# Two splits of the next token group one slot earlier, and four more units in the other product order, in a fused attention + two-MLP kernel

## The chip, the core and the metric

The kernel runs on one core of a Trainium2 chip. TensorE (PE) does the matrix products, ScalarE (ACT), VectorE (DVE) and GpSimd (POOL) do the work between them, SyncE (SP) issues the DMAs. The metric is the device time of one execution in microseconds; less is better.

## The reference, cut to what matters

```python
def _attn_ref(q, k, v):                       # 4 batches, 8 heads, 576 tokens, head size 64
    ...                                       # attention inside chunks of 64 tokens
    attn = np.exp(scores)
    attn = attn / (np.sum(attn, axis=-1, keepdims=True) + 1e-09)
    out = np.matmul(attn, v_c)
...
def _moe_ref(x, w_in, w_out):                 # x: 2304 x 512; w_in: 512 x 2048
    h = np.maximum(x @ w_in, 0.0)
    return (h * h @ w_out).astype(np.float32)
...
def _moe2_ref(x, domain_probs, w1, w2):       # 4 experts, w1[e]: 512 x 1024, w2[e]: 1024 x 512
    ...
    for e in range(E):
        h = np.maximum(x @ w1[e], 0.0)
        out += p[:, e:e + 1] * (h @ w2[e])
```

The attention output is the first MLP's input, and that MLP's output is the input of the four experts.

## The kernel before, in words

Attention and the first MLP fill roughly the first 485 us. The change lies in the last part, the experts.

**Split numbers.** A float32 operand is kept as a high part (a cast to fp32r, on ACT) and a low part (operand minus high part, on POOL or DVE), and a product is three matmuls: high by high, high by low, low by high.

**Units and slots.** The tokens are three groups of 768, each the left and right half of a 2x2 block matrix. A unit is 256 hidden columns of one expert for one group: 16 units a group, n = 0 to 47. From unit 7 on each layer uses Strassen's scheme (in Winograd's form), with seven products in place of eight. A unit has seven slots, u = 0 to 6, written here as (n, u). In slot (n, u) PE first runs one first-layer product of unit n (`c_unit`, line 609: 6 matmuls of 384 columns) and then three second-layer products (`d_unit`, line 710: 9 matmuls of 256 columns), of unit n-1 where u is 1 to 6 and the last three of unit n-2 where u is 0. So a slot is 15 matmuls.

**First layer.** The seven token operands (Y11, Y21, Y22, T1 to T4) stand split in seven places of one buffer. `UNITS` fixes their use: slot 0 takes Y11, then Y21, T2, T1, T3, Y22, T4. For a new group each place must be rewritten after the last unit of the old group (n = 15, 31) read it and before the first unit of the new one does. `SPLITS` says after which slot that is done: a key below 7 is a slot of the group's last unit, a key from 7 on is slot key-7 of the unit after. The rewrite (`y_split`) is an ACT cast at line 425 and a subtraction at line 427, on DVE for Y11, Y21, Y22 and on POOL for T1 to T4.

**Second layer.** The hidden block is turned into A11, A12, A22 and sums S1 to S4. The splits of the sums are an ACT cast (line 634) and a POOL subtraction (line 635); S2 itself is made by POOL (line 666). `PRODUCTS` lists the seven products; (t, k) in `SLOTS` is product k for token tile t of 3. Products 1, 2, 3, 5 of a tile go to one PSUM bank, 4, 6, 7 to another. DVE or ACT empty those banks in the middle of the accumulation: "B" (lines 763, 765) reads the bank of 6 and 7 before product 4 is added to it, "A" (line 767) reads the bank of 1 and 5 before products 2 and 3 are added to it. `AFTER` and `AFTER_ONCE` say after which slot each is recorded.

**The other product order.** A unit whose number is in `ONCE` takes `SLOTS_ONCE` and `AFTER_ONCE`: tile 0 and tile 1 begin with product 1 in place of product 7, so that the low part of S3 and S2 is asked for one product (3 matmuls) later; and of tile 2, products 6 and 1 come one slot later, with B and A of tile 2 both recorded after slot 6 in place of slots 5 and 6.

**Order.** The instruction streams of all engines are written out by hand in the loop at lines 1009 to 1081 (`manual_schedule`); each engine runs its own stream in order, and semaphores hold an instruction until what it reads is there and what it overwrites has been read. In a slot the order of recording is: `c_unit`, the unit's `c_finish`, `d_unit`, the moves, and last the splits.

Of the kernel before, what the change touches and what calls it, by code (L numbers as in the profile page):

```python
# [48 lines left out]
def tile_kernel(ctx, tc, q, k, v, moe_w_in, moe_w_out, moe2_p, moe2_w1, moe2_w2, out):  # L49
# [328 lines left out]
    Y11, Y21, Y22, T1, T2, T3, T4 = range(7)  # L378
# [43 lines left out]
    def y_split(sp, i):  # L422
        h, l = y_slot(i)
        a = comb[sp][i]
        nc.scalar.copy(h, a)
        eng = nc.vector if sp == 0 or i in (Y11, Y21, Y22) else nc.gpsimd
        eng.tensor_tensor(out=l, in0=a, in1=h.bitcast(F32), op=ALU.subtract)  # L427
        yield
# [267 lines left out]
        ((0, 5), (1, 5), (0, 4)), ((1, 4), (0, 2), (0, 3)), ((1, 2), (1, 3), (2, 7)),  # L696
        ((2, 1), (2, 6), (2, 5)),
    )
    ONCE = (9, 10, 13)
    pb = {}  # L700

    def d_unit(n, t, k):
        si, wi, x, c = PRODUCTS[k]
        if k in (1, 7):
            pb[n, t, x] = bank("a")
        p = pb[n, t, x][:, c * 2 * P:(c + 1) * 2 * P]
        hi, lo = (y[:, t * P:(t + 1) * P] for y in g[n][si])
        bh, bl = (y[:, wi] for y in w2c[n])
        for z, (w, y) in enumerate(((hi, bh), (hi, bl), (lo, bh))):
            nc.tensor.matmul(  # L710
                p, lhsT=w, rhs=y, start=(k in (1, 7) and z == 0), stop=(k in (3, 4) and z == 2),
                skip_group_check=True,
            )
# [107 lines left out]
    }  # L821
    AFTER_ONCE = {**AFTER, 5: ((1, "O"),), 6: ((2, "B"), (2, "A"))}
    ENDS = (3, 4, 0, 1, 5, 2)
    SPLITS = {1: Y11, 3: T2, 4: T1, 5: Y21, 8: T3, 9: Y22, 10: T4}

# [37 lines left out]
    with tc.manual_schedule():  # L865
# [44 lines left out]
        def run(chunks, n=None):  # L910
            while n is None or n > 0:
                try:
                    next(chunks)
                except StopIteration:
                    return
                n = None if n is None else n - 1
# [92 lines left out]
        for n in range(NQ + 2):  # L1009
# [5 lines left out]
            for u in range(7):  # L1015
# [54 lines left out]
                for d, at_ in ds:  # L1070
                    if 0 < at_ < 8:
                        for t, k in (SLOTS_ONCE if d in ONCE else SLOTS)[u]:
                            d_unit(d, t, k)
                    for t, what in (AFTER_ONCE if d in ONCE else AFTER if d < NQ - 2 else FLUSH).get(at_, ()):
                        d_move(d, t, what)
                if n < NQ and u == 4:
                    low(n, A22, st[n, "c"][:, :HALF])
                for back in (0, 1):
                    s1, m1 = divmod(n - back, NU)
                    if n >= back and m1 == NU - 1 and s1 + 1 < NSUP and u + 7 * back in SPLITS:  # L1080
                        run(y_split(s1 + 1, SPLITS[u + 7 * back]))

# [24 lines left out]
```

## Time and profile before

| what | value |
|---|---|
| median of 3 runs | 1200.18 us (1200.11 to 1201.43) |
| the profiled execution: time | 1208.68 us |
| the profiled execution: span of its instructions | 1206.9 us |
| mean granted TensorE clock | 0.994 |
| PE busy | 1185.9 us, 98% of the span |
| DVE, POOL, ACT busy | 841.1, 730.0, 610.4 us |

The span is from the first to the last instruction. A busy PE means that a matmul is in flight; how far apart matmuls start is seen in counts for a stretch and in the start times of a timeline.

### The profile page before, as it was taken

The numbers are of one execution on the slowest core, as the hardware profiler recorded it, in microseconds if no ns is written. First come the engines' busy times: TensorE is split into PE (matmuls) and PEld (weight loads), VectorE is DVE, ScalarE is ACT, GpSimd is POOL, SyncE is SP. The second block draws the span as 40 slices with busy tenths as digits, with TensorE's granted clock in tenths as the row PEclk, the third lists the DMA queues.
The fourth block names the chain that finished last, engine by engine and source line by source line (L and its number), as shares of the span: only waits on it lengthen the run. The fifth ranks groups of instructions, "written<-read, shape, count | busy, mean of one in ns | idle before, by whom it ended". The sixth has DMA issues, their size and how long they took to land.

```text
span 1206.9 us, 21703 instructions
## 1 busy us (share of the span) xinstructions
PE 1185.9 (98%) x8128; PEld 1110.9 (92%) x8128; DVE 841.1 (70%) x1400; ACT 610.4 (51%) x1250; POOL 730.0 (60%) x715
## 2 busy tenths in 40 slices
PE   6799999999999999999999999999999999999998
PEld 5788889888988988988899999999999999999997
DVE  6975665667667676456576778676767786767686
ACT  5655555454455444644354556454545554545543
POOL 3410047676675868777266678666766775656665
PEclk8999999999999999999999999999999999999999
DMA  9955132872964686566766667666666677666661
GB/s 208 198 116 128 44 99 79 278 252 81 327 213 149 217 272 226 201 224 239 291 258 245 247 253 289 257 250 254 249 254 250 252 281 276 262 266 251 246 262 53
DMA packets 142249, 265.43 MB, mean 220 GB/s; under 512 B 65344, under 2 KB 116544, under 8 KB 136000
## 3 DMA queue, kind: packets, MB, share of 16 engines
q1 hardware_dynamic: 139520, 263.39, 62.4%
q8 instruction: 64, 1.05, 0.3%
q10 hardware_dynamic: 2624, 0.66, 0.3%
q14 instruction: 41, 0.34, 0.1%
HBM read 200.58 MB, written 63.44 MB: 219 GB/s over the span
## 4 chain that ended last, share of the span: by engine, by line
PE 93%; DVE 2%; POOL 2%; DMA 1%; issue 1%; ACT 1%; SPq 0%; ACTq 0%; DVEq 0%; POOLq 0%
PE pst L609 23%; PE psa L710 22%; PE psa L336 17%; PE pst L303 10%; PE psh L303 7%; PE psa L727 6%; PE psh L609 4%; PE pst L279 1%; PE pst L238 1%; PE pst L223 1%; DMA v<-in_v 1%; POOL ar L427 1%; PE pst L265 1%; DMA q<-in_q 0%; POOL o L779 0%
## 5 line engine op out<-in xcount | busy, mean ns | idle before, releaser
L609 PE MATMUL pst<-ar 128*128 128x384 f32 x1728 | 347.5, 337 | 0.0
L609 PEld LDWEIGHTS pst<-ar 128*128 128x128 f32 x1728 | 292.1, 188 | 3.6
L336 PE MATMUL psa<-ar 128*128 128x512 f32 (+1 forms) x960 | 218.0, 371 | 0.0
L635 POOL TENSOR_TENSOR ar<-s,ar 128x384 fp32r<-128x384 f32 x160 | 163.3, 1033 | 68.3 <-ACT ar L634 65.2
L336 PEld LDWEIGHTS psa<-ar 128*128 128x128 f32 x960 | 173.8, 188 | 23.1 <-DVE acc L353 0.2
L710 PE MATMUL psa<-w2x,ar 128*128 128x256 f32 x1260 | 169.4, 279 | 0.3 <-POOL ar L635 0.3
L710 PE MATMUL psa<-ar 128*128 128x256 f32 x1260 | 169.0, 279 | 0.6 <-ACT uw L763 0.6
L710 PEld LDWEIGHTS psa<-ar 128*128 128x128 f32 x1260 | 164.7, 188 | 0.9 <-ACT uw L763 0.8
L710 PEld LDWEIGHTS psa<-w2x,ar 128*128 128x128 f32 x1260 | 164.8, 188 | 0.7 <-POOL ar L635 0.6
L779 POOL TENSOR_TENSOR o<-o,x 128x256 f32<-128x256 f32 x114 | 89.4, 784 | 88.5 <-ACT x L775 88.5
L148 POOL TENSOR_TENSOR raw<-raw 128x512 f32<-128x512 f32 x32 | 34.9, 1089 | 171.6 <-DVE raw L147 73.3
L303 PE MATMUL pst<-ar 128*128 128x512 f32 (+1 forms) x576 | 127.2, 369 | 0.0
L634 ACT CAST ar<-s 128x384 fp32r<-128x384 f32 x160 | 82.1, 513 | 81.8 <-DVE s L630 75.1
L642 ACT COPY u<-pst 128x384 f32<-128x384 f32 x144 | 69.5, 483 | 97.8 <-PE pst L609 96.0
L303 PEld LDWEIGHTS pst<-ar 128*128 128x128 f32 x576 | 105.4, 188 | 14.3
L767 DVE TENSOR_TENSOR uw<-psa,uw 128x512 f32<-128x512 f32 x120 | 79.2, 687 | 50.4 <-PE psa L710 29.9
L653 ACT ACTIVATE ar<-psh 128x384 fp32r<-128x384 f32 x96 | 47.3, 492 | 121.8 <-DVE psh L649 67.8
L303 PE MATMUL psh<-ar 128*128 128x512 f32 (+1 forms) x384 | 89.7, 376 | 2.1 <-DVE ar L287 2.1
L303 PEld LDWEIGHTS psh<-ar 128*128 128x128 f32 x384 | 69.1, 190 | 10.7 <-DVE ar L287 2.3
L765 DVE TENSOR_TENSOR uw<-psa,uw 128x512 f32<-128x512 f32 x87 | 59.9, 688 | 23.4 <-PE psa L710 22.1
L485 POOL TENSOR_TENSOR jsplit<-jraw,jsplit 128x448 fp32r<-128x448 f32 x44 | 54.7, 1249 | 35.3 <-ACT jsplit L483 31.0
L476 POOL TENSOR_TENSOR jraw<-jraw 128x256 f32<-128x256 f32 x88 | 70.1, 817 | 1.8
(139 smaller groups left out, 1943.9 us busy)
## 6 DMA issues: line engine op xcount, KB each, us to landing
ar<-w1d SPq DMA_DIRECT2D x41, 1792.0 KB, 7.3
w2x<-w2d SPq DMA_DIRECT2D x40, 896.0 KB, 8.0
ar<-w2d SPq DMA_DIRECT2D x40, 896.0 KB, 8.3
w2d<-jsplit SPq DMA_DIRECT2D x64, 448.0 KB, 4.2
w1d<-ar SPq DMA_DIRECT2D x7, 1792.0 KB, 8.7
w1d<-jsplit SPq DMA_DIRECT2D x24, 448.0 KB, 3.9
raw<-in_moe_w_in SPq DMA_DIRECT2D x16, 512.0 KB, 5.6
raw<-in_moe_w_out SPq DMA_DIRECT2D x16, 512.0 KB, 5.3
```

The source lines that it names most:

```text
L303: nc.tensor.matmul(ph[:, :T], lhsT=w[:, kk, :], rhs=x[tb][:, kk, :], start=(kk == 0 and n == 0), stop=(kk == KD - 1 and n == 2),)
L336: nc.tensor.matmul(o, lhsT=w, rhs=y, start=(f == 0 and n == 0), stop=(f == G - 1 and n == 2))
L476: nc.gpsimd.tensor_tensor(out=r[:, o], in0=r[:, a], in1=r[:, b], op=op)
L609: nc.tensor.matmul(p, lhsT=w[:, kk, :], rhs=y[:, kk, :], start=(kk == 0 and z == 0 and u in (0, 1, 3)), stop=(kk == 1 and z == 2 and u in ...
L634: nc.scalar.copy(h, st[n, nm])
L635: nc.gpsimd.tensor_tensor(out=l, in0=st[n, nm], in1=h.bitcast(F32), op=ALU.subtract)
L642: nc.scalar.copy(s, d if at == 3 else b)
L710: nc.tensor.matmul(p, lhsT=w, rhs=y, start=(k in (1, 7) and z == 0), stop=(k in (3, 4) and z == 2), skip_group_check=True,)
L727: nc.tensor.matmul(p, lhsT=w[:, ts], rhs=y[:, i, :], start=(i == 0 and z == 0), stop=(i == 1 and z == 2))
L765: nc.vector.tensor_tensor(out=uw, in0=b, in1=uw, op=ALU.add)
L767: nc.vector.tensor_tensor(out=uw, in0=pb[n, t, 0], in1=uw, op=ALU.add)
L779: nc.gpsimd.tensor_tensor(out=o1[:, :2 * P], in0=o1[:, :2 * P], in1=x, op=ALU.add)
```

## The change: what it does

```diff
-    ONCE = (9, 10, 13)
+    ONCE = (9, 10, 13, 17, 18, 33, 34)
...
-    SPLITS = {1: Y11, 3: T2, 4: T1, 5: Y21, 8: T3, 9: Y22, 10: T4}
+    SPLITS = {1: Y11, 2: T2, 3: T1, 5: Y21, 8: T3, 9: Y22, 10: T4}
```

No instruction is added or removed on any engine. Four things move, each at both group boundaries (units 15 and 31): the splits of T2 and T1, and the second-layer products and moves of units 17, 18 (and 33, 34).

POOL's stream in unit 15 (acc_1090 holds T1 and T2; x is a scaled output piece that line 779 adds to the output tile; lines 666 and 635 begin the S2 and S3 of unit 15):

```order
 L635 TENSOR_TENSOR ar<-s_7371,ar 128x384
 L787 TENSOR_TENSOR o<-o,x_7385 128x512
-L427 TENSOR_TENSOR ar<-acc_1090,ar 128x768
-L779 TENSOR_TENSOR o<-o,x_7459 128x256
-L427 TENSOR_TENSOR ar<-acc_1090,ar 128x768
-L779 TENSOR_TENSOR o<-o,x_7485 128x256
+L427 TENSOR_TENSOR ar<-acc_1090,ar 128x768 x2
+L779 TENSOR_TENSOR o<-o,x_7461 128x256
+L779 TENSOR_TENSOR o<-o,x_7487 128x256
 L666 TENSOR_TENSOR s_7502<-s_7498,a_7399 128x384
 L635 TENSOR_TENSOR ar<-s_7500,ar 128x384
```

The second subtraction passes the first addition; both splits stand ahead of both additions.

ACT's stream in the same unit (acc_1963 holds Y11; line 642 copies a first-layer bank, 653 and 657 make A22):

```order
 L425 CAST ar<-acc_1963 128x768
 L642 COPY u_7424<-pst 128x384
-L642 COPY u_7446<-pst 128x384
-L775 ACTIVATE x_7459<-psa,prob 128x256
 L425 CAST ar<-acc_1090 128x768
-L653 ACTIVATE ar<-psh 128x384
-L657 ACTIVATE a_7473<-psh 128x384
-L775 ACTIVATE x_7485<-psa,prob 128x256
+L642 COPY u_7448<-pst 128x384
+L775 ACTIVATE x_7461<-psa,prob 128x256
 L425 CAST ar<-acc_1090 128x768
```

T2's cast moves ahead of the copy and the scaled move of slot 3; T1's moves ahead of the two activations and the scaled move of slot 4.

PE's stream in slots 1 to 3 of unit 18, which run the second layer of unit 17 (each psa number is one bank; before, tile 0's bank of products 7 and 6 is psa_7950, after it is psa_7954):

```order
 L609 MATMUL psh_7935<-ar_79 128x384 x6
-L710 MATMUL psa_7950<-w2x_6022,ar_79 128x256 x6
-L710 MATMUL psa_7957<-w2x_6022,ar_79 128x256 x3
-L609 MATMUL pst_7910<-ar_79 128x384 x6
-L710 MATMUL psa_7971<-w2x_6022,ar_79 128x256 x6
-L710 MATMUL psa_7978<-w2x_6022,ar_79 128x256 x3
-L609 MATMUL pst_7983<-ar_79 128x384 x6
-L710 MATMUL psa_7957<-w2x_6022,ar_79 128x256 x3
-L710 MATMUL psa_7978<-w2x_6022,ar_79 128x256 x3
 L710 MATMUL psa_7950<-w2x_6022,ar_79 128x256 x3
+L710 MATMUL psa_7954<-w2x_6022,ar_79 128x256 x6
```

The product that needs no sum (k = 1) now opens the slot, and products 7 and 6 follow it.

## Rows read from the trace of the kernel before

**Rows 1.** Windows: stretch, length; then busy us (matmuls) of PE, PEld, DVE, ACT, POOL.

```profile
740.00:960.00 220.00, 220.00 (x1558) 220.00 (x1557) 159.37 (x268) 112.88 (x254) 146.08 (x147) 1.00 0.67 256
990.00:1190.00 200.00, 200.00 (x1458) 200.00 (x1458) 145.92 (x248) 103.90 (x234) 125.82 (x135) 1.00 0.64 247
```

**Rows 2.** Timeline, PE, 722 to 731: start, length, what; idle time before it.

```profile
721.73 1.19 PE L710 MATMUL psa<-ar 128*128 128x256 f32 x9
722.75 1.20 PE L609 MATMUL pst<-ar 128*128 128x384 f32 x6
...
725.85 0.73 PE L710 MATMUL psa<-w2x,ar 128*128 128x256 f32 x5
726.85 0.74 PE L710 MATMUL psa<-w2x,ar 128*128 128x256 f32 x4 [0.27 <-POOL ar L635]
727.43 1.22 PE L609 MATMUL pst<-ar 128*128 128x384 f32 x6
```

**Rows 3.** Timeline, PE, 960 to 968.

```profile
963.81 1.47 PE L710 MATMUL psa<-w2x,ar 128*128 128x256 f32 x9
965.11 1.20 PE L609 MATMUL pst<-ar 128*128 128x384 f32 x6
```

**Rows 4.** Timeline, PE, 980 to 989.

```profile
982.63 0.85 PE L710 MATMUL psa<-ar 128*128 128x256 f32 x6
984.06 0.62 PE L710 MATMUL psa<-ar 128*128 128x256 f32 x3 [0.58 <-ACT uw L763]
```

**Rows 5.** Timeline, POOL, 700 to 740.

```profile
714.62 2.02 POOL L787 TENSOR_TENSOR o<-o,x 128x512 f32<-128x512 f32 x1
718.10 1.85 POOL L427 TENSOR_TENSOR ar<-acc,ar 128x768 fp32r<-128x768 f32 x1 [1.45 <-ACT ar L425]
...
720.61 1.85 POOL L427 TENSOR_TENSOR ar<-acc,ar 128x768 fp32r<-128x768 f32 x1
...
723.84 1.01 POOL L666 TENSOR_TENSOR s<-s,a 128x384 f32<-128x384 f32 x1
724.81 2.96 POOL L635 TENSOR_TENSOR ar<-s,ar 128x384 fp32r<-128x384 f32 x3
```

**Rows 6.** Timeline, ACT, 705 to 735.

```profile
717.19 0.82 ACT L425 CAST ar<-acc 128x768 fp32r<-128x768 f32 x1
```

**Rows 7.** Timeline, DVE, 714 to 732.

```profile
722.16 1.12 DVE L427 TENSOR_TENSOR ar<-acc,ar 128x768 fp32r<-128x768 f32 x1
723.20 0.68 DVE L767 TENSOR_TENSOR uw<-psa,uw 128x512 f32<-128x512 f32 x1
```

**Rows 8.** Source line 803, DVE: duration ns min/median/max.

```profile
L803 DVE SCALAR_TENSOR_TENSOR o<-uw,prob,o x27: 735/843/3890, 622.0 to 1197.7; 128x512 f32<-128x512 f32 x27
```

**Rows 9.** Timeline, POOL, 950 to 990.

```profile
976.45 1.99 POOL L635 TENSOR_TENSOR ar<-s,ar 128x384 fp32r<-128x384 f32 x2
...
980.07 0.72 POOL L779 TENSOR_TENSOR o<-o,x 128x256 f32<-128x256 f32 x1
```

**Rows 10.** Timeline, DVE, 972 to 986.

```profile
977.46 3.89 DVE L803 SCALAR_TENSOR_TENSOR o<-uw,prob,o 128x512 f32<-128x512 f32 x1
```

**Rows 11.** Timeline, PE, 707 to 713.

```profile
709.23 1.33 PE L710 MATMUL psa<-w2x,ar 128*128 128x256 f32 x9
710.39 1.20 PE L609 MATMUL psh<-ar 128*128 128x384 f32 x6
```

**Rows 12.** Timeline, PE, 662 to 670.

```profile
665.84 1.30 PE L710 MATMUL psa<-ar 128*128 128x256 f32 x9
666.98 1.20 PE L609 MATMUL psh<-ar 128*128 128x384 f32 x6
668.01 1.19 PE L710 MATMUL psa<-w2x,ar 128*128 128x256 f32 x9
```

**Rows 13.** Timeline, PE, 648 to 655.

```profile
650.92 1.30 PE L710 MATMUL psa<-w2x,ar 128*128 128x256 f32 x9
652.06 1.22 PE L609 MATMUL psh<-ar 128*128 128x384 f32 x6
```

## The prediction

> **What bounds the kernel now.** I read the page first: PE is busy for 98% of the span (table above), so an edit pays only where PE waits or where its matmuls start farther apart than they could. In the expert part the waits are few, so I went on to PE's timeline slot by slot and compared start times.
>
> Three waits stand out. In slot (16,1) the second-layer part runs from 725.85 to the next slot's start at 727.43, 1.58 us against the 1.02 of the slot before (721.73 to 722.75); the timeline names POOL's line 635, and by its place (after five of nine matmuls) it is the low part of S2 of unit 15 [rows 2]. In (32,1), one group later, the same part takes 1.30, where 1.06 is usual around it (below) [rows 3]. In (33,3) its first six matmuls take 1.43, some 0.75 too long by six ninths of 1.02, and the wait is for ACT's copy at line 763 [rows 4].
>
> The second thing is larger. Between 740 and 960 PE ran 1558 matmuls in 220 us, between 990 and 1190 it ran 1458 in 200 us, both without a gap, at a granted clock of 1.00 [rows 1]. Per slot of 15 matmuls that is 2.118 against 2.058 us. The instructions have the same shapes. So PE has two paces, 0.060 us a slot apart, and the change from one to the other happens at a short wait: before (16,1) the second-layer part of a slot took 1.02; 0.060 is 0.004 a matmul, so nine take 1.06 at the slow pace, and that stays so for 237.7 us (727.43 to 965.11, 112 slots), until the wait in (32,1), behind which the quick pace is back [rows 2, 3]. Also slow to quick went it in slot (12,0), where 1.14 is followed by a first-layer part of 1.03 [rows 12]. (11,0) lost 0.08 and stayed slow, (15,0) lost 0.14 and stayed quick, (33,3) lost 0.75 and stayed quick [rows 13, 11, 4]. The rows show that a wait can change the pace, not what decides it.
>
> **T2 and T1 one slot sooner.** POOL goes into the boundary late: it ends line 787 at 714.62 + 2.02 = 716.64 and then stands idle 1.45 us until ACT's cast of T2 is there (717.19 + 0.82 = 718.01) [rows 5, 6]. From 718.10 it works through: two subtractions of 1.85, the additions of line 779 (0.72 us undisturbed [rows 9]), S2's making at 723.84, and then three subtractions of 0.99 each from 724.81, of which S2's is the second and ends at 726.79, where PE goes on at 726.85 [rows 2, 5]. After the change T2's cast needs only its own place free, which slot (15,2) has read by 713.5 (it starts five slots of 2.06 before 722.75, and its first-layer part takes 1.04 [rows 2]), and T1's cast takes the place at 717.19 that T2's had. So POOL's first subtraction starts at 716.64, the second at 718.45 (its cast is there at 718.01), two additions end near 721.7, and S2 can be made some two microseconds sooner; DVE's S1, which it needs, is made before DVE turns to the split at 722.16 [rows 7]. S2's low part is 1.3 to 2.2 us sooner, against a lateness of 0.56. Both waits go: 0.56 + 0.24 = **-0.80 us**. ACT's two casts cost nothing: ACT is idle for about half of the span (table).
>
> What is late next? In (16,0), product (2,2) overwrites what the move A (line 767) of tile 2 reads, and A stands behind DVE's split of Y21 (722.16, 1.12 us); it ends at 723.88 [rows 7]. The second-layer part of (16,0) starts one slot before 725.85, at 723.79 [rows 2], and (2,2) is three matmuls in, at 724.13. The cover is 0.25 us, less the release. In the profiled run DVE's subtraction waited for POOL's second one to end (720.61 + 1.85 = 722.46) and ran some 0.82 from there [rows 5, 7]. With POOL ahead, it would find the making of S2 (1.01) under way and start near 722.65, ending 0.19 later: a loss of 0 to 0.2 us a boundary, of which I take 0. DVE can wait longer: line 803, also with two operands in SBUF, took 3.89 us in place of 0.84, from 977.46 to 981.35, while POOL ran one instruction after the other from 976.45 to 980.79 [rows 8 to 10]. I use that for a rival.
>
> The Trainium skill, "SBUF — State Buffer", "Who interferes with whom", says that a VectorE instruction with two SBUF inputs contends with a GpSimd one that reads SBUF, and that the later of the two is blocked until the first is done. It speaks against moving POOL's work under that split. By it the wait is one POOL instruction and the sum is as above; the 3.89 us at line 803 reaches over several, so trace and page differ on how long it can be.
>
> **Four units in the other order.** The order relieves POOL's S3 and S2 by three matmuls (0.34 us). Units 17, 18, 33, 34 show no wait there: slots (18,1), (19,1), (34,1) and (35,1) lie in the two stretches in which PE was busy throughout [rows 1]. So nothing is won. What it costs is seen at the units that have it: B and A of tile 2 now both follow slot 6, and (2,4) and (2,2) wait for them in the next unit's slot 0. Unit 9 lost 0.08 in (11,0), unit 10 0.08 in (12,0), unit 13 0.14 in (15,0) (1.16 against 1.02) [rows 11 to 13]. Four more of them, in (19,0), (20,0), (35,0), (36,0): 0.3 to 0.6, I take **+0.45 us**.
>
> **The pace.** If the wait in (16,1) is gone, what sent PE into the slow pace is gone, and the slots to (32,1) keep the quick one: 112 x 0.060 = **-6.7 us**. The new short waits in (19,0) and (20,0) come in the same place of a slot as those that left a quick pace quick once (15,0) and turned a slow one quick once (12,0), so they favour it. The bounds are 0 (the pace turns slow anyway, or never was) and -6.7.
>
> The wait in (33,3) follows from the 3.89 us above, since the copy it waits for stands behind DVE's late work; POOL's shift moves it out of that coincidence or not. 0 to -0.75, I take 0.
>
> **Sum.** -0.80 + 0.45 - 6.7 = -7.05. The profiled execution took 1208.68 us, so it would be 1201.6. The three runs shown have a median of 1200.18, 8.5 us below the profiled one; taking off the same microseconds gives **1193.1 us**. Its own range is 1192.2 (the (33,3) wait gone too, 0.3 for the orders) to 1194.9 (0.6 for the orders, and quick only from (20,0) on, 26 slots later). I call within 0.2% (2.4 us) no change, about what a measurement of this kernel can tell.
>
> **Rivals.** First, **the pace does not change**: the sum is -0.35, 1199.8 us. For it: the runs shown are 8.5 us shorter than the profiled one. Slow slots there add up to 6.7 us in units 16 to 32, and there are more before (12,0) (650.92 to 665.84 is 14.92 us for seven slots with one loss of 0.08, so 2.12 each [rows 12, 13]); if the runs shown had none of them, there is nothing to win. Against it: the profiled run's early part, loading weights, can as well be what is longer. The Trainium skill, "TensorE: Matmul & The Clock Gate", "Back-to-back issue gap", gives the spacing by the number of columns alone; by that rule there would be no second pace and this would be the result, but [rows 1] show two for the same columns. Chance 0.36.
>
> Second, **slower, the pace turns the other way**: one of the new waits in (35,0) or (36,0) does in the last group what (16,1) did, quick to slow. From (36,0) to the end of unit 46 are 77 slots, +4.6 us; with the third quarter as it was, 1200.18 - 0.35 + 4.6 = 1204.4. It decides as soon as more slots turn slow than quick by 46 (2.4 us plus 0.35). For it: one of three waits met in quick pace did that [rows 2, 4, 11]; against it, the other order's own wait in (15,0) did not. Chance 0.11.
>
> Third, **slower, DVE is starved** at the split of Y21 as at line 803: 3.89 from 722.16 ends at 726.05, A at 726.7, and (2,2) starts 2.6 us late, at two boundaries 5.2; without a gain in pace 1200.18 - 0.35 + 5.2 = 1205.0. It decides once it costs more than 1.4 us a boundary. For it, POOL now runs without a break from 716.64; against it, the split waited for one POOL instruction alone before [rows 5, 7]. Chance 0.08.
>
> **Numbers.** Forecast 0.45, no change of pace 0.36, slower 0.11 + 0.08. Forecast is faster by over 0.2%, the second within, the others slower: 0.45, 0.36, 0.19. Two cases of different sign hold most of the chance, so the range has both, from 1191.0 (1192.2 less the 1.3 us by which the three runs differ, rounded) to 1202.5 (the upper end of no change), and leaves out the slower ones.
>
> **What will show it.** Right: in (16,1) and (32,1) PE's second-layer part takes 1.02 with no wait for line 635; POOL's line 427 starts near 716.6 and 718.4 in place of 718.1 and 720.6 (counted from the same slot); slots of 2.06 from unit 16 to 32; waits of about 0.1 in (19,0), (20,0), (35,0), (36,0). Wrong: slots of 2.12 over that stretch again, or in units 36 to 46; a wait of PE for line 767 or 763 in (16,0) or (32,0); a DVE line 427 of over 2 us in unit 15 or 31; or a trace as forecast and a time that has not moved, which would say that the pace of the profiled execution is not that of the runs.

## The result

In its first timing the changed kernel was slower: a median of 1206.08 us over 11 runs (1203.0 to 1210.7) against 1200.11 for before (1197.22 to 1201.82), ratio 1.0053 with an interval of 1.0043 to 1.0063. A gain of 0.6% was forecast. Yet the profiled execution of the changed kernel (1204.86 us, one of the 11) is shorter than the one the prediction was worked out from (1208.68). That one lies 7 us above every run of before in this timing. Most of what sets either of them apart from later traces of its kernel is PE's pace, as the sum below shows; the sign of the first timing did not come back in the later ones.

The page of the changed kernel, busy time by engine:

```profile
PE 1185.6 (99%) x8128; PEld 1110.8 (92%) x8128; DVE 839.3 (70%) x1400; ACT 610.9 (51%) x1250; POOL 731.2 (61%) x715
```

PE is busy as before, 99% of the span (98% there). Its timeline at the boundary, the changed kernel's answer to [rows 2] (all slots here start 2.9 us earlier than there):

```profile
719.87 1.20 PE L609 MATMUL pst<-ar 128*128 128x384 f32 x6
720.90 1.31 PE L710 MATMUL psa<-ar 128*128 128x256 f32 x9
722.05 1.21 PE L609 MATMUL psh<-ar 128*128 128x384 f32 x6
723.10 1.20 PE L710 MATMUL psa<-w2x,ar 128*128 128x256 f32 x9
724.14 1.20 PE L609 MATMUL pst<-ar 128*128 128x384 f32 x6
...
729.30 1.29 PE L710 MATMUL psa<-w2x,ar 128*128 128x256 f32 x9
730.43 0.85 PE L609 MATMUL pst<-ar 128*128 128x384 f32 x4
```

The second-layer part of (16,1) runs from 723.10 to 724.14, 1.04 us where it was 1.58: the wait for line 635 is gone, as forecast. Two small ones have come. (16,0) takes 1.15 (720.90 to 722.05) and (16,4) 1.13 (729.30 to 730.43), where 1.02 is usual. POOL and DVE show why, in the order POOL, then DVE:

```profile
711.74 2.02 POOL L787 TENSOR_TENSOR o<-o,x 128x512 f32<-128x512 f32 x1
713.71 3.69 POOL L427 TENSOR_TENSOR ar<-acc,ar 128x768 fp32r<-128x768 f32 x2
717.33 1.46 POOL L779 TENSOR_TENSOR o<-o,x 128x256 f32<-128x256 f32 x2
718.71 1.05 POOL L666 TENSOR_TENSOR s<-s,a 128x384 f32<-128x384 f32 x1
...
726.29 1.85 POOL L427 TENSOR_TENSOR ar<-acc,ar 128x768 fp32r<-128x768 f32 x1
```

```profile
719.28 1.31 DVE L427 TENSOR_TENSOR ar<-acc,ar 128x768 fp32r<-128x768 f32 x1
720.51 0.68 DVE L767 TENSOR_TENSOR uw<-psa,uw 128x512 f32<-128x512 f32 x1
...
727.12 1.84 DVE L427 TENSOR_TENSOR ar<-acc,ar 128x768 fp32r<-128x768 f32 x1 [0.37 <-ACT ar L425]
728.88 1.28 DVE L767 TENSOR_TENSOR uw<-psa,uw 128x512 f32<-128x512 f32 x2
```

POOL's two splits run back to back from 713.71, 4.14 us after (15,2) starts at 709.57; in [rows 5] it was 5.65 (718.10 against 712.45), and the forecast was 4.19. (The prediction's 718.45 and 722.65 go by 1.81 us from one start to the next, not by the 1.85 that it prints; the trace has 3.62 for the two splits.) DVE's split of Y21 takes 1.31 in place of 1.12, so A ends at 721.19 and PE's (2,2) waits some 0.1 for it. The split of Y22 that is recorded after (16,2) (727.12, 1.84 us) runs beside POOL's split of T3 (726.29), and the moves A of tiles 0 and 1 behind it are late for (16,4). Each of these DVE splits ends 0.82 to 0.83 us after the POOL instruction that was under way when it began (719.76 to 720.59, 728.14 to 728.96; before, 722.46 to 723.28), which fits a wait for that one instruction and no more; the third rival's 3.89 us did not come. The first of these two waits was in the prediction with 0 to 0.2 us, the second was not in it.

Now the pace. Windows of the changed kernel (the columns of [rows 1], then granted clock, DMA share and GB/s):

```profile
735.00:763.00 28.00, 28.00 (x206) 28.00 (x205) 22.23 (x37) 15.35 (x35) 17.55 (x18) 1.00 0.83 313
780.00:1000.00 220.00, 220.00 (x1558) 220.00 (x1558) 162.05 (x271) 114.91 (x257) 149.98 (x150) 1.00 0.67 257
1030.00:1175.00 145.00, 145.00 (x1057) 145.00 (x1056) 108.72 (x184) 75.13 (x170) 91.51 (x99) 1.00 0.67 258
```

1057 matmuls in 145 us are 2.058 us a slot, 1558 in 220 us are 2.118: the same two paces, to the third digit. The slow stretch has moved. It begins and ends here:

```profile
763.39 1.20 PE L609 MATMUL pst<-ar 128*128 128x384 f32 x6
764.42 1.34 PE L710 MATMUL psa<-w2x,ar 128*128 128x256 f32 x9
765.60 1.22 PE L609 MATMUL psh<-ar 128*128 128x384 f32 x6
766.66 1.22 PE L710 MATMUL psa<-ar 128*128 128x256 f32 x9
767.72 1.22 PE L609 MATMUL pst<-ar 128*128 128x384 f32 x6
```

```profile
1001.00 1.22 PE L609 MATMUL pst<-ar 128*128 128x384 f32 x6
1002.06 1.30 PE L710 MATMUL psa<-w2x,ar 128*128 128x256 f32 x9
1003.20 1.20 PE L609 MATMUL psh<-ar 128*128 128x384 f32 x6
1004.24 1.19 PE L710 MATMUL psa<-ar 128*128 128x256 f32 x9
1005.26 1.02 PE L609 MATMUL pst<-ar 128*128 128x384 f32 x5
```

The first-layer part of (19,0) takes 1.03 (763.39 to 764.42), that of (19,1), behind the wait that unit 17's new order brings (1.18 in place of 1.02), 1.06. The wait of unit 33's order in (35,0) turns it back: 1.06 ahead of it (1001.00 to 1002.06), 1.04 behind. In between lie 112 slots.

### The profile page after: what moved, and what is told of

It is laid out like the page before. It is cut to its first block, busy times and chain, and to the rows that moved or that the text cites. A ratio compares the mean times of both kernels' runs of the same rounds, so it can differ in the third digit from the quotient of the medians.

```text
span 1203.1 us, 21705 instructions
## 1 busy us (share of the span) xinstructions
PE 1185.6 (99%) x8128; PEld 1110.8 (92%) x8128; DVE 839.3 (70%) x1400; ACT 610.9 (51%) x1250; POOL 731.2 (61%) x715
## 3 DMA queue, kind: packets, MB, share of 16 engines
q8 instruction: 64, 1.05, 0.3%
## 4 chain that ended last, share of the span: by engine, by line
PE 96%; DMA 1%; DVE 1%; issue 0%; ACT 0%; ACTq 0%; SPq 0%; DVEq 0%
PE pst L609 25%; PE psa L710 24%; PE psa L336 17%; PE pst L303 10%; PE psh L303 6%; PE psa L727 6%; PE psh L609 4%; DMA k<-in_k 1%; PE pst L279 1%; PE pst L238 1%; PE pst L223 1%; PE pst L265 0%; PE psa L279 0%; PE psa L223 0%; DVE e L245 0%
```

## The experiments

Each timing from the second on ran on a chip of its own, beside runs of before on that chip; on which the first ran is not on record. Medians in us, range in brackets:

| timing | before | kernels |
|---|---|---|
| first | 1200.1 (1197.2 to 1201.8), 11 runs | changed 1206.1 (1203.0 to 1210.7) |
| second | 1199.8 (1197.3 to 1203.2), 29 | splits alone 1199.3 (1197.4 to 1214.3), orders alone 1200.4 (1199.3 to 1202.4), changed without 33, 34: 1201.5 (1198.9 to 1212.4) |
| third | 1199.6 (1197.9 to 1202.3), 18 | changed 1200.3 (one run), tile 2 as usual 1212.2 (1199.5 to 1214.4), changed without 17, 18: 1206.0 (1197.7 to 1215.5), fewer waits 1206.2 (1204.9 to 1212.4) |
| fourth | 1206.2 (1198.0 to 1214.9), 35 | changed 1200.7 (1199.6 to 1203.4), wait put back 1202.3 (1199.3 to 1204.8), tiles 0 and 1 with old splits 1205.4 (1197.4 to 1212.3), moved at 15 only 1201.1 (1199.8 to 1202.4) |
| fifth | 1199.3 (1197.2 to 1208.0), 23 | changed 1198.7 (1197.7 to 1201.7), splits alone 1201.2 (1197.3 to 1206.0) |
| sixth | 1199.8 (1197.3 to 1205.9), 23 | changed 1199.8 (1197.5 to 1202.0), orders alone 1200.6 (1198.1 to 1204.7) |
| seventh | 1199.4 (1198.2 to 1204.4), 23 | changed 1200.3 (1198.4 to 1202.7), tile 2 as usual 1200.6 (1197.5 to 1204.8) |

**The second timing: which part of the change?** The kernel before once more, then each part alone, then the changed kernel without half of its reordered units:

```diff
 splits alone:                 ONCE = (9, 10, 13)
                               SPLITS = {1: Y11, 2: T2, 3: T1, 5: Y21, ...}
 orders alone:                 ONCE = (9, 10, 13, 17, 18, 33, 34)
                               SPLITS = {1: Y11, 3: T2, 4: T1, 5: Y21, ...}
 changed without 33, 34:       ONCE = (9, 10, 13, 17, 18)
                               SPLITS = {1: Y11, 2: T2, 3: T1, 5: Y21, ...}
```

> The kernel before, profiled once more. The page that the prediction rests on took 1208.68 us, above all eleven runs of before (1197.2 to 1201.8). If its slow stretch of 112 slots was that execution's own, this one takes about 1200 us and PE keeps slots of 2.06 us through units 16 to 32 (pace theory: the shown execution was an odd one). If the runs are shorter for another reason (the early part), the slots there are 2.12 us again and the loss lies before 485 us.

It took 1199.64. Its windows, to set against [rows 1]:

```profile
740.00:960.00 220.00, 219.73 (x1599) 219.53 (x1598) 163.23 (x276) 117.57 (x262) 152.01 (x154) 1.00 0.70 265
990.00:1180.00 190.00, 190.00 (x1384) 190.00 (x1384) 139.33 (x237) 97.51 (x220) 119.99 (x129) 1.00 0.63 241
```

1599 matmuls where the first profile of before has 1558, in the same 220 us: no slow slot, though the waits of 0.53 in (16,1) and (32,1) are there. So the execution from which the prediction was made is not what before usually did: no run of the first timing is over 1202, and one of 29 in this timing is over 1203.

> T2 and T1 one slot sooner, the product orders as before. Pace theory (the short waits that the other order brings in (19,0), (20,0), (35,0), (36,0) turn the pace, and that is the 6 us): no such waits here, so the time is that of before or up to 0.8 us less, ratio 0.999 to 1.001, and units 17 to 31 of 14.42 us. Split theory (POOL's work one slot sooner makes DVE's split of Y21 late, and the new wait in (16,0) turns or delays PE): the whole loss, ratio about 1.005. Plain sum of waits: ratio 0.999 to 1.000.

Ratio 1.0003 (0.998 to 1.0026): eleven of the twelve executions lie at 1197.4 to 1200.1, one at 1214.3. Split theory falls; what costs 15 us in that one execution had no trace.

> Units 17, 18, 33, 34 in the other order, the splits as before. Pace theory: the wait in (19,0) or (20,0) turns PE slow until a later wait turns it back ((32,1) or (35,0)), so some 91 to 112 slots of 0.060, ratio 1.004 to 1.006, and units 20 to 31 of 14.84 us in the trace. Split theory: ratio 1.000. Plain sum of waits: four of 0.08 to 0.14 us, ratio 1.0004.

Ratio 1.0006 (0.9995 to 1.0017). Its four new waits are in the trace, some 0.1 each, and none of them turned the pace for longer than a slot. So the waits of the new order need not do what they did in the changed kernel's first trace: pace theory, as stated here, was too simple.

> The changed kernel with 33 and 34 back in the usual order. Pace theory: the wait in (19,0) or (20,0) turns PE slow, and the waits in (35,0) and (36,0) that turned it back in the changed kernel's trace are gone, so it stays slow to unit 46 unless another wait turns it: up to 27 units of 0.42 us, 11 us, ratio up to 1.010, in no case below that of the changed kernel (1.005). Plain sum of waits: half of the changed kernel's four waits, so less than the changed kernel, ratio 1.000 to 1.003.

Ratio 1.0027 (1.0007 to 1.0047), executions from 1198.9 to 1212.4. It is not above the changed kernel's 1.0053, against pace theory as stated. The one with a trace, 1201.62, turned quick in (12,0) and behind that was slow for no more than a slot; what made others take up to 1212.4 is not known.

**The third timing: without the waits.** The order of tile 2 kept, half of the reordered units, and a version with fewer waits:

```diff
 tile 2 as usual:   +SLOTS_EARLY = SLOTS[:1] + SLOTS_ONCE[1:3] + SLOTS[3:]   # for 17, 18, 33, 34
 without 17, 18:     ONCE = (9, 10, 13, 33, 34)
 fewer waits:        ONCE = ()
                     SPLITS = {1: Y11, 2: T2, 3: T1, 4: Y21, 7: Y22, 8: T3, 10: T4}
```

> The changed kernel, profiled once more. Pace theory: its time lies in the range of its eleven runs (1203 to 1211 us) and the excess over 1199 us is in the expert part as slots of 2.12 us between one short wait and another, some 70 to 190 of them; the first of these slots follows a short wait, and its place is not the one of the first trace (units 19 to 35) by necessity. Plain sum of waits: all slots of 2.06 us and the excess in single waits of PE.

Pace theory had it in the range of the first timing and misses: it took 1200.27, below all eleven. Units 17 to 46 ran at 14.42 to 14.57 us, but for unit 32 (14.68) with its two waits. The changed kernel can be as quick as before.

> The changed kernel, but units 17, 18, 33, 34 take the other order for tiles 0 and 1 alone; tile 2 and its moves B and A keep their slots, so PE doesn't wait for A in (19,0), (20,0), (35,0), (36,0). Pace theory: no such waits, no turns of the pace beyond those of the splits alone, ratio 0.998 to 1.001. If the order of the products itself (banks, weights) costs, the ratio is that of the changed kernel, 1.005.

A miss for both theories: median 1212.22, ratio 1.0083 (1.0053 to 1.0113), with none of the four waits. Its timeline in unit 16:

```profile
730.25 1.20 PE L609 MATMUL pst<-ar 128*128 128x384 f32 x6
731.28 1.31 PE L712 MATMUL psa<-w2x,ar 128*128 128x256 f32 x9
732.43 1.22 PE L609 MATMUL pst<-ar 128*128 128x384 f32 x6
733.49 1.22 PE L712 MATMUL psa<-w2x,ar 128*128 128x256 f32 x9
734.55 1.22 PE L609 MATMUL pst<-ar 128*128 128x384 f32 x6
```

The small wait in (16,4) (731.28 to 732.43) turned the pace: first-layer parts of 1.03 ahead, 1.06 behind. From there to unit 46 no slot has a wait, and none is quick.

> The changed kernel with 17 and 18 back in the usual order, so that of the new waits of slot 0 only (35,0) and (36,0) are left, with at most 83 slots behind them. Pace theory: at most 83 x 0.060 = 5 us over before, in some of the executions, ratio 1.000 to 1.004. Plain sum of waits: ratio 0.999 to 1.000.

Ratio 1.0054 (1.0019 to 1.0088): six executions at 1197.7 to 1200.7 and six at 1211.3 to 1215.5, nothing between. Pace theory allowed 5 us and misses. The profiled one, 1212.99, is slow in all 280 slots from unit 8 to the last, so from before the first wait that the change touches; its windows:

```profile
740.00:960.00 220.00, 220.00 (x1560) 220.00 (x1559) 159.44 (x269) 112.56 (x253) 147.84 (x149) 1.00 0.67 255
990.00:1180.00 190.00, 190.00 (x1346) 189.97 (x1346) 134.83 (x229) 95.11 (x215) 114.25 (x123) 1.00 0.66 255
```

> A version that should beat both: T2 and T1 one slot sooner as in the change, DVE's split of Y21 one slot sooner still (so that the move A of tile 2 isn't behind it and (16,0) has no wait), the split of Y22 two slots sooner (so that the moves A after slot 3 aren't behind it and (16,4) has no wait), and no unit in the other order, so no wait in (11,0), (12,0), (15,0) either. Pace theory: hardly a wait is left that can turn the pace, so nearly all executions lie at the quick end, 1196.5 to 1199 us, ratio 0.997 to 0.999, and the spread is smaller than before's. Plain sum of waits: 0.8 + 3 x 0.12 less, ratio 0.999. If the moved splits of Y21 and Y22 make DVE late elsewhere, waits show at line 609 or 710 in units 16 and 32, ratio over 1.

A miss: ratio 1.0064 (1.0046 to 1.0082). DVE's split of Y22, put two slots sooner, makes A11 late and with it POOL's split of T3; the waits of PE between 600 and 1180 us:

```profile
PE pst L609 <- POOL ar L427: 2.1, 2, 1.1
PE psa L710 <- DVE uw L767: 0.3, 2, 0.2
```

Without the waits that unit 9's and 10's order bring in (11,0) and (12,0) the slow pace with which it came out of the plain units lasted to (16,0).

**The fourth timing: is it the lost wait?** In the traces so far a slow PE had come back in (32,1) of the first profile, and the changed kernel has no wait there. So the next theory was that the change takes away what ends a slow stretch.

```diff
 wait put back (in y_split):   for _ in range(2 if sp > 0 and i == T1 else 1):
                                   eng.tensor_tensor(out=l, in0=a, in1=h..., op=ALU.subtract)
 tiles 0, 1, old splits:       SLOTS_EARLY as above, SPLITS = {1: Y11, 3: T2, 4: T1, ...}
 moved at 15 only:             sl = SPLITS if s1 == 0 else SPLITS_LAST      # SPLITS_LAST: as before
```

> The changed kernel, but POOL does the low part of T1 twice (the same values again), 1.85 us in each of units 15 and 31, so that S2 of those units is late again and PE waits in (16,1) and (32,1) as before. Reset theory (a short wait of about 0.1 us can throw PE into the slow pace; the wait of 0.25 us that a slow PE meets in (16,1) and (32,1) puts it back; the change took that wait away, so a slow stretch now lasts): executions over 1206 us vanish though work and a wait are added, ratio 0.999 to 1.002. If instead the four units in the other order are what counts, the ratio stays that of the changed kernel in this call; if added work is only added, it is that plus 0.0007.

Ratio 0.9978 (0.9951 to 1.0005), but the changed kernel itself had no execution over 1206 in this timing, so the times tell nothing of a reset. The trace does: PE turned slow in (32,0), and the wait of 0.56 in (32,1) left it slow, against reset theory.

> The kernel before with units 17, 18, 33, 34 in the other order for tiles 0 and 1 alone, splits as before. With the splits moved this had a median of 1212 us, with slots of 2.12 from (16,5) to the end. Reset theory: with the old splits the waits in (16,1) and (32,1) are there, so slow stretches end: ratio 0.999 to 1.002, no execution over 1206. If the product order of tiles 0 and 1 was the cause: ratio 1.006 to 1.010.

Ratio 0.9992 (0.9957 to 1.0027), so the order of tiles 0 and 1 by itself is not the cause. Reset theory falls here, since with the old splits six of twelve executions lie over 1206, up to 1212.3. The profiled one (1208.78), first in unit 16, then in unit 32:

```profile
725.76 1.20 PE L609 MATMUL psh<-ar 128*128 128x384 f32 x6
726.80 0.73 PE L712 MATMUL psa<-w2x,ar 128*128 128x256 f32 x5
727.80 0.74 PE L712 MATMUL psa<-w2x,ar 128*128 128x256 f32 x4 [0.27 <-POOL ar L635]
728.38 1.22 PE L609 MATMUL pst<-ar 128*128 128x384 f32 x6
729.43 1.22 PE L712 MATMUL psa<-w2x,ar 128*128 128x256 f32 x9
```

```profile
963.70 1.22 PE L609 MATMUL psh<-ar 128*128 128x384 f32 x6
964.75 1.49 PE L712 MATMUL psa<-w2x,ar 128*128 128x256 f32 x9
966.08 1.20 PE L609 MATMUL pst<-ar 128*128 128x384 f32 x6
967.12 1.19 PE L712 MATMUL psa<-w2x,ar 128*128 128x256 f32 x9
```

The long wait in (16,1) is what threw PE into the slow pace (1.04 ahead of it, 728.38 to 729.43 is 1.05 behind and 1.06 the slots after), and that in (32,1) brought it back: the same two turns as in the first profile of before.

> The changed kernel beside the others on this chip. Eleven runs had a median of 1206.1, a single later one took 1200.3 with all slots of units 13 to 46 quick. Reset theory: executions of both kinds, some at 1199 to 1201, some at 1203 to 1214, none of them much below 1198.5; ratio 1.002 to 1.008, with a wider spread than before's.

Ratio 0.9976 (0.9952 to 1.0000): here it is before that spreads, 11 executions at 1198.0 to 1202.1, 19 at 1205.7 to 1208.7 and 5 at 1212.7 to 1214.9. Steps of some 7 us are what one and two groups of units in the slow pace would cost (112 x 0.060 = 6.7); no execution of before has a trace from this chip. The changed kernel has twelve at 1199.6 to 1203.4, against reset theory, which gave it the wider spread.

> The changed kernel with T2 and T1 split sooner at the boundary of unit 15 alone; at unit 31 they are split as before, so the wait in (32,1) is back, that in (16,1) is not. Reset theory: a slow stretch that begins at (16,0) or later ends in (32,1) (112 slots, 6.7 us), so executions lie between 1199 and 1207, none above 1208 except for one that turns slow in (35,0) or (36,0) again (5 us), ratio 1.000 to 1.005, below that of the changed kernel.

Ratio 0.9985 (0.9966 to 1.0005), all twelve at 1199.8 to 1202.4. The executions lie where reset theory had them, the ratio a little below. But in the profiled one (32,1), which by that theory puts PE back, threw it, and (35,0) brought it back.

**The fifth to seventh timing: is the sign the change's or the chip's?** The changed kernel on three more chips, each time with one other.

> The changed kernel beside before on one more chip. Chip theory (whether a short wait throws PE into the slow pace differs from chip to chip and from execution to execution, for each kernel apart): the ratio here is anywhere from 0.993 to 1.008 and its sign need not be that of the first timing; each kernel's executions lie at 1197 to 1203 or some 7 us (one group of units slow) or 14 us above. Change theory (the reordered units make the changed kernel slow): ratio 1.003 to 1.008 again.

Ratio 0.9986 (0.9965 to 1.0006). Change theory fails. Chip theory's 0.993 to 1.008 would have held almost any result, so that it held is weak support.

> The splits alone on the same chip. Chip theory: its quick executions lie 0 to 0.8 us below before's quick ones (on the first chip 1197.4 to 1200.1 against 1197.3 to 1203.2), and where before has executions near 1206 it has fewer of these, since the waits in (16,1) and (32,1) that throw PE are gone, but the few that are slow stay slow to the end, near 1213. Change theory: ratio 0.999 to 1.001, whatever the changed kernel does.

Ratio 1.0010 (0.9986 to 1.0033), six executions at 1197.3 to 1199.7 and six at 1202.8 to 1206.0. Five of its twelve are over 1203 where before has six of 23, so not fewer, against what was expected; none is near 1213.

> The changed kernel beside before on a further chip. Chip theory: ratio between 0.993 and 1.008 with either sign; each kernel's profiled execution obeys time = start of unit 8 + 0.060 us x slow slots + PE's waits + 591.7 us within 0.3 us. Change theory: ratio 1.003 to 1.008.

Ratio 0.9996 (0.9981 to 1.0011), below change theory again. The profiled execution took 1202.02; the remainder in the next section's sum is 591.61.

> The reordered units alone on the same chip. Its waits in (16,1) and (32,1) are those of before, and it has four more of 0.1 us. Chip theory: executions at 1199 to 1202 where the chip seldom throws PE, else also some 7 us above; median within 0.3% of before's on the same chip. If the reordered units are what made the changed kernel slow: ratio 1.003 or more.

Ratio 0.9998 (0.9980 to 1.0015): the reordered units alone are not slower.

> The changed kernel beside before on one more chip. Chip theory: as on the last three, 0.997 to 1.001, or as in the first timing, 1.003 to 1.008 with all executions over 1203, if the chip throws it. Change theory: 1.003 to 1.008.

Ratio 1.0004 (0.9992 to 1.0016), below change theory a third time.

> The kernel that had a median of 1212 us on the second chip, beside before on another. Chip theory: a different share of its executions is slow here, and the median lies between 1198 and 1208; where one is slow it is so to the end, 1209 to 1215, since it has neither the waits of (16,1) and (32,1) nor those of slot 0. Program theory: median 1209 or more again.

Ratio 1.0005 (0.9992 to 1.0017). The kernel with six of seven executions over 1203 on the third timing's chip has two of twelve here. Program theory falls. Chip theory had slow executions at 1209 to 1215; the two took 1204.3 and 1204.8, and the first of them, the profiled one, went slow to the end only in (32,0).

## Why the prediction was wrong

**One sum for every execution.** For each of the 20 profiled executions (11 kernels) I counted in PE's timeline, from unit 8 to the end, the slots at the slow pace (S), and added up what PE's matmuls started late in waits (W, with the last unit's). Time is then the start of unit 8 plus 0.060 x S plus W plus a remainder:

| execution | time | unit 8 starts | S | W | remainder |
|---|---|---|---|---|---|
| before, first profile | 1208.68 | 606.40 | 141 | 2.24 | 591.58 |
| before, again | 1199.64 | 606.07 | 0 | 1.72 | 591.85 |
| changed, first profile | 1204.86 | 603.85 | 138 | 1.19 | 591.54 |
| changed, third timing | 1200.27 | 605.25 | 31 | 1.38 | 591.77 |
| changed, sixth timing | 1202.02 | 604.15 | 86 | 1.09 | 591.61 |
| orders alone, second timing | 1199.26 | 605.08 | 5 | 2.15 | 591.74 |
| tile 2 as usual, third timing | 1212.61 | 605.53 | 248 | 0.58 | 591.63 |
| without 17, 18 | 1212.99 | 604.10 | 280 | 0.50 | 591.59 |

Over all 20 the remainder lies between 591.5 and 591.9. So to 0.4 us nothing but S, W and the start tells one execution from another, and S is the largest of the three: 0 to 280 slots are 0 to 16.8 us, W differs by 3.7 us at most (by 2.4 without the version with fewer waits), the start by 3.5.

**Right: what the change does to the waits.** POOL's splits start 4.14 us after (15,2), forecast 4.19; the waits for line 635 are gone; the other order brings its 0.08 to 0.16 us in (19,0), (20,0), (35,0), (36,0). In quick executions the sum of waits is -2 x 0.53 + 4 x 0.105, and + 2 x (0.08 + 0.09) for (16,0), (16,4), (32,0), (32,4), that is -0.30; -0.35 was forecast for all that is not pace. On the last four chips' timings the ratio of the changed kernel is 0.9976, 0.9986, 0.9996 and 1.0004: what the first rival gave (1199.8), not the forecast.

**Wrong: the term of the pace, -6.7 us.** The step that failed is "taking off the same microseconds". The term was read in one execution and taken off the median of others. The 8.5 us by which the profiled execution lay above that median are as much as its own slow slots cost (141 x 0.060 = 8.5). The second trace of before, 1199.64, has no slow slot, and runs that have none cannot win them; the three runs themselves have no trace. The first rival said so and I held its chance below the forecast's. The wait in (33,3), too, stands in none of the other 19 traces.

The premise under it failed as well: "what sent PE into the slow pace is gone". In the 20 traces, from unit 8 to 46, and counting a turn where the pace is another two slots later: of 99 waits below 0.2 us that met a quick PE, 5 turned it slow; of 40 that met a slow one, 19 turned it quick. Of 20 longer ones (0.24 to 1.4 us) 16 met a quick PE and turned it 4 times, 4 met a slow one and turned it 3 times. Without a wait no turn lasted in any trace. So each wait is a draw, and the change swaps two long draws for eight short ones. Four of the eight are the splits' own, in (16,0), (16,4), (32,0), (32,4), which the sum put at 0 or did not have. Over all versions that have them short, 4 of 37 that met a quick PE turned it slow, against 3 of 10 of the old long ones in (16,1) and (32,1).

The odds differ by place, and by what is not known: a slow PE came out quick from the wait in (12,0) in 10 of 12 traces, from the like one in (11,0) in 3 of 15. That the waits of the other order "favour" the quick pace, argued from one turn and one wait without a turn, is borne out as odds: in (19,0), (20,0), (35,0), (36,0) they met a quick PE 33 times and turned it slow once, a slow one 11 times and turned it quick 6 times. That once is (19,0) in the changed kernel's first profile. So for that execution the second rival was right in kind (it had (35,0)), by a draw that was unlikely.

**What stays open.** Ten of the changed kernel's 11 runs in the first timing lie over 1203, one of 48 in the five later timings that had it. Before has none of 11, then 1 of 29, 0 of 18, 24 of 35, 6 of 23, 4 of 23 and 2 of 23. Shares so far apart within one kernel suggest that something which holds for a timing (its chip, or how the program lies there) weights the draws. Each chip of the later timings was used in one, so these two are not told apart, and by what means they act was not tried. Only one of the changed kernel's 11 runs has a trace, so why ten of them lay over 1203 stays open. The first timing's 0.5% is a fact of that timing; as a statement on the change it did not come back in five later ones, one of them a single run.

The Trainium skill, "TensorE: Matmul & The Clock Gate", "Back-to-back issue gap", gives, at one clock level, one spacing for a number of columns. The trace differs: 2.058 and 2.118 us for the same 15 matmuls, at a granted clock of 1.00 in both stretches.

## What to carry to other kernels

Before a profile is taken as the kernel, set its time beside the runs: one that lies above all of them shows an execution of another kind, and its excess must be found in the trace before it is forecast away. Where PE has no gaps, count matmuls per window as well: two stretches of the same shapes with 1558 and 1599 in 220 us were worth more than all waits together. And where executions of one kernel fall into groups 7 us apart, a difference of 0.5% on one chip can be a draw; compare the groups, and on more chips.

## What was not expected of the hardware

PE runs a stream of equal matmuls at one of two steady paces, 0.004 us a matmul apart (2.118 and 2.058 us for 6 of 384 and 9 of 256 columns), stayed in the slow one for up to 280 slots, and changed over for more than two slots only at a wait, a wait of 0.07 us being enough. What holds it in a pace is not known. The kernel before had 24 of 35 executions over 1203 us on one chip, on another none of 18.
